# First loads of a windowed-attention and SiLU feed-forward kernel: q/k rows in four loads with a shared leftover tile, v blocks in two, the first w_in chunk in halves

## The chip, the cores and the metric

The kernel runs on one core of a Trainium2 chip. The metric is the device time of one launch in microseconds: 320.09 us, the median of six runs (318.83 to 320.32). The core has the engines PE (TensorE, matmuls and transposes), DVE (VectorE), ACT (ScalarE), POOL (GpSimd) and SP (SyncE). They run side by side, each in the order of its own program, and wait for each other by semaphores. Loads are moved by 16 DMA engines; here nearly all loads are issued by POOL, since they also turn f32 into f16.

## The reference

```python
B, H, S, D = 8, 8, 576, 64
scores = 1/sqrt(D) * q @ k.T
rel = pos[:, None] - pos[None, :]
mask_plain = (rel >= 0) & (rel < 32)                        # heads 0..3
mask_dil = (rel >= 0) & (rel < 128) & (rel % 4 == 0)        # heads 4..7
attn_out = softmax(masked scores) @ v
x = attn_out.transpose(0, 2, 1, 3).reshape(4608, 512)
h = x @ w_in                    # 512 x 2048
g = h * 1/(1 + exp(-h))
out = g @ w_out                 # 2048 x 512, f32
```

q, k and v are f32 of shape (8, 8, 576, 64). A query sees 32 keys: the last 32 tokens in a plain head, and every fourth of the last 128 in a dilated one.

## The kernel before

**Tiling.** Each batch has 576 tokens. Plain heads work on six blocks of 96 queries (`QB`), each with 128 keys (32 older and its own). Dilated heads see the tokens as m x 4 (`M` = 144 values of m, `DIL` = 4 residues), in two halves of 72 queries with 128 keys each. Layer 1 of the feed-forward (`h`, line 877) and layer 2 (`y`, line 910) go over groups of 512 tokens (the first 512 in two groups of 256), in f16 with f32 accumulation.

**First three batches.** q and k come as rows with m on partitions. 144 rows don't fit on 128 partitions, so they come as 96 (`MA`) and 48 (`MR`). PE transposes them (`td` for dilated heads, `ta` for plain ones), ACT or DVE copies the result out of PSUM to `kqD`, `kP` and `qP`, and PE makes the scores. From batch 3 on, q and k take another path (through DRAM and transposing DMAs) that the change doesn't touch.

**First batch.** Its loads are written out apart from the others. For k, rows 0 to 95 go to the tile `nat` "k", for q, rows 48 to 143 go to `nat` "q" and rows 0 to 47 to `q_rest`, a view of the tile `xR` 1 that is not otherwise used so early. Dilated heads are issued first (`issue_first(HN, H)`), then identity and band mask are made on POOL, then the plain heads' rows are issued. The k rows 96 to 143 follow later (`k0`, to `nat` "rest"). The v data come in two forms: `vraw`, rows for the dilated heads, in two loads (the second is `r0`), and `vp`, 24 windows of 128 tokens for the plain heads, in seven loads: one window without its first 32 rows, the three others of block 0, and then one load for each of the blocks 1 to 5 (3 to 5 are `v0`). `trans_d0`, `trans_a0` make the scores' operands of the first rows, `trans_d1`, `trans_a1` those of the leftover k rows. The first batch's mask is added on PE by a matmul with the band (line 611).

**Order.** `ORDER` is the order in which POOL issues everything behind these: w_in in four chunks of 512 columns (w0 to w3), batch 1's rows (d1 dilated, p1 plain), its v (r1, v1), and w_out in four pieces (o0 to o3). `c0` is a copy on POOL of the second half of `vraw`. POOL issues a load only when the load eight places before it has landed. The order of PE, ACT and DVE is written by a planner inside the kernel (`Plan`): it starts each step when its rings (PSUM buffers) and due times are ready by its own estimates. The due times come from `LOAD_US` (us for each load), `AT_W0` (when the loads ahead of w_in's stage are in), and the tables `AT_DIL`, `AT_PLAIN`, `AT_VRAW`, `AT_VP`. On the chip each engine simply waits in that order.

Of the kernel before, what the change touches and what calls it, by code (L numbers as in the profile page):

```python
# [9 lines left out]
F16 = mybir.dt.float16  # L10
# [6 lines left out]
def kernel(  # L17
# [9 lines left out]
    nc = tc.nc  # L27
    B, H, S, D = q.shape
    DM, DFF = moe_w_in.shape
    P = 128  # L30
# [24 lines left out]
    ORDER = "k0 r0 v0 w0 w1 c0 w2 w3 d1 p1 r1 o0 v1 o1 o2 o3".split()  # L55
    LOAD_US = {"w": 2.55, "o": 2.55, "d": 3.7, "p": 3.7, "r": 1.4, "v": 2.6, "k0": 0.9, "r0": 1.2, "v0": 2.0, "c0": 0.0}
    AT_W0 = 14.5
# [48 lines left out]
    def nat_of(b, key):  # L106
        i = ("k", "q", "rest").index(key)
        return nats[b % 2][:MA, i * RW : (i + 1) * RW].rearrange("p (h r d) -> p h r d", h=H, r=DIL)
# [5 lines left out]
    def issue_nat(b, h0, h1):  # L114
# [10 lines left out]
    q_rest = xRs[1][:MA].rearrange("p c t -> p (c t)").rearrange(  # L125
        "p (h r d) -> p h r d", h=H, r=DIL
    )

    def issue_part(src, m0, m1, dst, h0, h1):
        rows = src[0].rearrange("h (m r) d -> m h (r d)", r=DIL)  # L130
        nc.gpsimd.dma_start(  # L131
            out=dst[: m1 - m0, h0:h1].rearrange("p h r d -> p h (r d)"), in_=rows[m0:m1, h0:h1]
        )

    def issue_first(h0, h1):
        issue_part(k, 0, MA, nat_of(0, "k"), h0, h1)
        issue_part(q, MR, M, nat_of(0, "q"), h0, h1)
        issue_part(q, 0, MR, q_rest, h0, h1)
# [32 lines left out]
    def v_win(t0, n, step=S * D):  # L171
        flat = v.rearrange("b h s d -> (b h s) d")
        win = flat[t0 : t0 + P]
        return bass.AP(
            tensor=win.tensor, offset=win.offset, ap=[win.ap[0], [step, n], win.ap[1]]
        )
# [4 lines left out]
    def issue_vp_first(half):  # L181
        flat = v.rearrange("b h s d -> (b h s) d")
        vp = vps[0].rearrange("p (h j) c -> p h j c", j=NB)
        if half == 0:
            nc.gpsimd.dma_start(out=vp[W:, 0, 0, :D], in_=flat[:QB])
            nc.gpsimd.dma_start(out=vp[:, 1:, 0, :D], in_=v_win(S - W, HN - 1))
        for j in (1, 2) if half == 0 else (3, 4, 5):
            nc.gpsimd.dma_start(out=vp[:, :, j, :D], in_=v_win(j * QB - W, HN))  # L188

    nc.vector.memset(xRs[1][:MA], 0.0)  # L190
    nc.vector.memset(vps[0][:W, 0, :], 0.0)
    for t in vraws:
        nc.vector.memset(t, 0.0)
    nc.vector.memset(nat_of(0, "rest"), 0.0)
    issue_first(HN, H)
    make_identity(nc, ident)
# [6 lines left out]
    issue_first(0, HN)  # L203
    issue_vraw(0, (0,))
    issue_vp_first(0)
# [5 lines left out]
    for t in vps:  # L211
        nc.vector.memset(t[:, :, D:], 1.0)
    for t in vds:
        nc.vector.memset(t[:, :, :, :, D:], 1.0)
    for t in kPs:
        nc.vector.memset(t[:, :, :W], 0.0)
    nc.vector.memset(kqDs[0][:, :, :, 1, MA:], 0.0)
# [5 lines left out]
    FC = 512  # L223
    wi = moe_w_in.rearrange("(c p) f -> p c f", p=P)
    wo = moe_w_out.rearrange("(c p) m -> p c m", p=P)
    AT = {}
    at = AT_W0
    for what in ORDER:
        kind, n = what[0], int(what[1:])
        if kind == "w":  # L230
            nc.gpsimd.dma_start(
                out=w_in16[:, :, n * FC : (n + 1) * FC], in_=wi[:, :, n * FC : (n + 1) * FC]
            )
        elif kind == "o":
            nc.gpsimd.dma_start(
                out=w_out16[:, 4 * n : 4 * n + 4], in_=wo[:, 4 * n : 4 * n + 4]
            )
        elif what == "k0":
            issue_part(k, MA, M, nat_of(0, "rest"), 0, H)
        elif what == "r0":  # L240
            issue_vraw(0, (1,))
        elif what == "v0":
            issue_vp_first(1)
        elif what == "c0":
            nc.gpsimd.tensor_copy(vds[0][:, 1, :, :, :D], vraws[0][:, 1])
        elif kind == "d":
            issue_nat(n, HN, H)
        elif kind == "p":
            issue_nat(n, 0, HN)
        elif kind == "r":  # L250
            issue_vraw(n)
        else:
            issue_vp(n)
        at += LOAD_US[what if n == 0 and kind in "krvc" else kind]
        AT[what] = at

# [85 lines left out]
    AT_DIL = {0: 6.7, 1: AT["d1"], 2: t2 + 7.0}  # L342
    AT_PLAIN = {0: 11.3, 1: AT["p1"], 2: t2 + 7.0}
    AT_VRAW = {0: 12.2, 1: AT["r1"], 2: t2 + 8.6}
    AT_VP = {0: 14.5, 1: AT["v1"], 2: t2 + 11.4}
    AT_CAST = t2 + 18.0
    AT_REST = AT["k0"]
    AT_V1 = (max(AT["r0"] + 1.2, 18.0), AT["v0"])
    AT_WIN = [AT[f"w{n}"] for n in range(4)]
# [97 lines left out]
    def attention(b):  # L447
# [34 lines left out]
        def kq_dil(n, i, h, rp, c, w):  # L482
            r = slice(i * D, i * D + D)
            if pe_path:
                return kqD[r, h, rp, n ^ (b == 0), c : c + w]
            return kqT[r, n, rp, h * M + c : h * M + c + w]
# [53 lines left out]
        def trans_d0(ring, h):  # L540
            tps = small(ring, [P, 2, MR + 2 * MA], F16, f"td_{b}_{h}")
            for rp in range(2):
                for c0, src in (
                    (0, q_rest), (MR, nat_of(b, "q")), (MR + MA, nat_of(b, "k"))
                ):
                    nc.tensor.transpose(  # L546
                        tps[:, rp, c0 : c0 + MA], src[:, HN + h, 2 * rp : 2 * rp + 2, :],
                        ident[:MA, :MA],
                    )
            step = best(0.40, 0.52)  # L550
            yield step
            copy_on(
                step[0], kqD[:, h].rearrange("p r k m -> p r (k m)")[:, :, : MR + 2 * MA], tps
            )

        def trans_d1(ring):
            tps = small(ring, [P, 2 * HN * MR + MR], F16, f"td1_{b}")
            for n in range(2 * HN):
                h, rp = divmod(n, 2)
                nc.tensor.transpose(  # L560
                    tps[:, n * MR : n * MR + MA],
                    nat_of(b, "rest")[:, HN + h, 2 * rp : 2 * rp + 2, :], ident[:MA, :MA],
                )
            tps = tps[:, : 2 * HN * MR].rearrange("p (h r m) -> p h r m", r=2, m=MR)
            step = best(0.36, 0.45)
            yield step
            copy_on(step[0], kqD[:, :, :, 1, MA:], tps)

        def trans_a0(ring, hp, nm):
            w = MA if nm == "k" else M  # L570
            tps = small(ring, [P, DIL, w], F16, f"ta_{b}_{hp}_{nm}")
            parts = [(0, nat_of(b, "k"))] if nm == "k" else [(0, q_rest), (MR, nat_of(b, "q"))]
            for r in range(DIL):
                for c0, src in parts:
                    for i in range(2):
                        nc.tensor.transpose(
                            tps[i * D : i * D + D, r, c0 : c0 + MA], src[:, 2 * hp + i, r, :],
                            ident[:MA, :MA],
                        )
            step = best(0.47, 0.42) if nm == "k" else best(0.68, 0.56)  # L580
            yield step
            dst = kP[:, hp, W : W + DIL * MA] if nm == "k" else qP[:, hp]
            copy_on(step[0], dst.rearrange("p (m r) -> p m r", r=DIL), tps.rearrange("p r m -> p m r"))

        def trans_a1(ring, hp):
            tps = small(ring, [P, DIL * MR + MR], F16, f"ta1_{b}_{hp}")
            for r in range(DIL):
                for i in range(2):
                    nc.tensor.transpose(
                        tps[i * D : i * D + D, r * MR : r * MR + MA],  # L590
                        nat_of(b, "rest")[:, 2 * hp + i, r, :], ident[:MA, :MA],
                    )
            tps = tps[:, : DIL * MR].rearrange("p (r m) -> p r m", r=DIL)
            step = best(0.28, 0.34)
            yield step
            dst = kP[:, hp, W + DIL * MA :].rearrange("p (m r) -> p m r", r=DIL)
            copy_on(step[0], dst, tps.rearrange("p r m -> p m r"))
# [172 lines left out]
        for key in order:  # L770
# [9 lines left out]
            elif kind == "TA" and b == 0:  # L780
                st = Step(
                    lambda ring, a=a: trans_a0(ring, *a), 0.75 if a[1] == "k" else 1.3, rings,
                    [AT_PLAIN[0]],
                )
            elif kind == "TD" and b == 0:
                st = Step(lambda ring, a=a: trans_d0(ring, *a), 0.25, rings, [AT_DIL[b]])
            elif kind == "TR":
                st = Step(lambda ring: trans_d1(ring), 0.2, rings, [AT_REST])
            elif kind == "TS":
                st = Step(lambda ring, a=a: trans_a1(ring, *a), 0.2, rings, [AT_REST])  # L790
# [27 lines left out]
            elif kind == "V":  # L818
                st = Step(lambda ring, a=a: vd_of(*a), 0.0, (), [AT_V1[0] if b == 0 and a[0] else at_vraw], ())
            elif kind == "P":  # L820
# [3 lines left out]
                    [AT_V1[1] if b == 0 and a[0] > 2 else at_vp] + [steps["S", u] for u in us], ("DVE",),  # L824
# [43 lines left out]
    def layer1(g, deps):  # L868
        w = GROUPS[g][1]

        def l1(ring, f):
# [4 lines left out]
            for c in range(HP):  # L876
# [18 lines left out]
                list(deps) + [AT_WIN[f // 4]], ("ACT", "DVE"),  # L895
# [123 lines left out]
```

The softmax here doesn't subtract the row's maximum and nothing guards it: scores larger than these inputs give would overflow.

## Time and profile before

| what | value |
|---|---|
| median of six runs | 320.09 us (318.83 to 320.32) |
| the profiled execution's own time, its span | 320.19 us, 318.5 us |
| granted TensorE clock, mean | 0.989 |
| busy: PE, DVE, ACT, POOL | 301.5, 196.1, 164.0, 57.9 us |
| first transpose, first matmul of layer 1 | 6.86, 20.93 us |
| wait before the first matmul of layer 1 | 2.18 us, for w_in |
| first matmul of layer 2 | 41.41 us, after 0.96 us of waiting for w_out |
| batch 2's first transposes | 57.74 us; 0.33 us of waiting at 58.28 |
| stretch at half clock | 21.6 to 28.5 us |

The profile is of one execution. The span goes from the first to the last instruction; the run's time is 1.7 us longer. All starts are in us from the beginning of the span. "Busy" of PE is modelled for overlapping matmuls, so it may be above the real load. An idle time is put down to what ended last before it. The granted clock is the share of PE's clock that the chip let through.

### The profile page before, as it was taken

How to read it: one execution, taken by the hardware profiler on the slowest of the kernel's cores; microseconds unless marked ns; L12 is line 12 of the kernel's file. 1: busy time of each engine (PE TensorE's matmuls, PEld its weight loads, DVE VectorE, ACT ScalarE, POOL GpSimd, SP SyncE). 2: the span in 40 equal slices, each digit the busy share in tenths (PEclk: the TensorE clock that was granted, in tenths of full speed). 3: DMA queues.
4: the chain of work that ended last, by engine and by line, in shares of the span. 5: the costliest groups of instructions: out<-in, count | busy, mean ns of one | idle time of the engine just before them, and what ended most of it. 6: DMA issues, size and time to landing. Idle time of an engine off the chain costs nothing.

```text
span 318.5 us, 6150 instructions
## 1 busy us (share of the span) xinstructions
PE 301.5 (95%) x2402; PEld 154.6 (49%) x2402; DVE 196.1 (62%) x493; ACT 164.0 (51%) x300; POOL 57.9 (18%) x92
## 2 busy tenths in 40 slices
PE   1978979999999999999999999999999999999994
PEld 1647856555545444544444454444444444444441
DVE  6437989698879768843895787548841552355000
ACT  6755766477765355443653564546452453355111
POOL 8972924000900041005000500000000000000000
PEclk9987999999999999999999999999999999999999
DMA  7999999999999959998999898952181000100221
GB/s 90 153 190 198 159 196 192 212 185 177 112 205 225 201 106 196 179 227 153 195 244 195 134 204 179 191 114 71 54 183 38 31 33 33 66 35 0 84 82 66
DMA packets 106693, 44.51 MB, mean 140 GB/s; under 512 B 73384, under 2 KB 102056, under 8 KB 106664
## 3 DMA queue, kind: packets, MB, share of 16 engines
q0 software_dynamic: 48528, 19.92, 51.8%
q1 hardware_dynamic: 52952, 14.75, 24.6%
q10 hardware_dynamic: 5184, 9.44, 8.8%
q8 instruction: 19, 0.31, 0.4%
q14 instruction: 10, 0.08, 0.1%
HBM read 39.84 MB, written 18.28 MB: 182 GB/s over the span
## 4 chain that ended last, share of the span: by engine, by line
PE 82%; DMA 10%; POOL 4%; issue 1%; DVE 1%; ACT 1%; POOLq 0%
PE y L910 37%; PE h L877 36%; DMA nat<-in_q_dram 5%; PE s L623 3%; DMA w_out<-in_moe_w_out_dram 3%; PE av_d L672 2%; DMA w_in<-in_moe_w_in_dram 2%; PE av_p L672 2%; POOL vp L188 1%; POOL nat L131 1%; POOL vraw L166 1%; DVE oD L676 0%; PE td L529 0%; POOL xR L131 0%; ACT th L886 0%
## 5 line engine op out<-in xcount | busy, mean ns | idle before, releaser
L910 PE MATMUL y<-w_out,gT 128*128 128x512 f16 x576 | 138.5, 379 | 1.3 <-DMA w_out<-in_moe_w_out_dram 1.3
L888 DVE SCALAR_TENSOR_TENSOR gT<-th,h 128x512 f16<-128x512 f32 (+1 forms) x160 | 98.3, 628 | 63.0 <-ACT th L886 62.9
L886 ACT ACTIVATE th<-h 128x512 f32<-128x512 f32 (+1 forms) x160 | 88.5, 555 | 85.9 <-PE h L877 81.1
L877 PEld LDWEIGHTS <-w_in 128*128 128x128 f16 x640 | 59.1, 98 | 55.8 <-DMA w_in<-in_moe_w_in_dram 2.3
L910 PEld LDWEIGHTS <-gT 128*128 128x128 f16 x576 | 53.7, 98 | 60.7 <-issue 1.5
L877 PE MATMUL h<-xR,w_in 128*128 128x512 f16 x320 | 77.9, 379 | 0.1
L877 PE MATMUL h<-xA,w_in 128*128 128x512 f16 (+1 forms) x320 | 66.2, 343 | 2.6 <-DMA w_in<-in_moe_w_in_dram 2.2
L921 ACT ACTIVATE ob<-y 128x512 f32<-128x512 f32 x36 | 21.5, 597 | 42.5 <-PE y L910 42.4
L632 ACT ACTIVATE probs<-s 128x768 f16<-128x768 f32 (+2 forms) x47 | 36.2, 771 | 12.6 <-PE s L623 10.0
L676 DVE TENSOR_TENSOR oD<-av_d,rcps 72x256 f16<-72x256 f32 x64 | 26.9, 421 | 2.2
L672 PEld LDWEIGHTS <-probs 128*128 128x128 f16 x448 | 21.9, 99 | 12.7 <-ACT probs L636 0.7
L676 DVE TENSOR_TENSOR oP<-av_p,rcps 96x256 f16<-96x256 f32 x48 | 20.2, 421 | 1.6
L408 POOL COPY fence<-kqT 128x1 f16<-128x1 f16 x10 | 2.4, 250 | 93.5 <-DMA kqT<-kq_s 93.5
L672 PE MATMUL av_d<-vd,probs 128*128 128x65 f16 x256 | 14.9, 196 | 1.5 <-DVE rcps L675 0.6
L675 DVE RECIPROCAL rcps<-av_p 96x4 f32<-96x4 f32 x48 | 8.3, 174 | 11.7 <-PE av_p L672 11.6
L675 DVE RECIPROCAL rcps<-av_d 72x4 f32<-72x4 f32 x64 | 11.0, 172 | 5.6 <-PE av_d L672 5.6
L641 DVE TENSOR_TENSOR probs<-probs,mask_p 128x768 f16<-128x768 f16 x21 | 11.6, 552 | 4.0 <-ACT probs L632 3.8
L672 PE MATMUL av_p<-vp,probs 128*128 128x65 f16 x192 | 13.0, 197 | 0.0
L641 DVE TENSOR_TENSOR probs<-probs,mask_d 128x576 f16<-128x576 f16 (+1 forms) x23 | 11.8, 513 | 1.0 <-ACT probs L632 0.8
L166 POOL DMA_DIRECT2D vraw<-in_v_dram x16 | 10.8, 678 | 5.6 <-DVE oD L676 2.1
L179 POOL DMA_DIRECT2D vp<-in_v_dram x7 | 10.3, 1474 | 1.9 <-PE h L877 1.8
L546 PE MATMUL td<-ident,xR 96*128 96x96 f16 x8 | 1.9, 276 | 6.9 <-DMA xR<-in_q_dram 6.9
(94 smaller groups left out, 155.0 us busy)
## 6 DMA issues: line engine op xcount, KB each, us to landing
out_dram<-ob ACTq DMA_DIRECT2D x36, 256.0 KB, 3.0
kq_s<-in_k_dram POOLq DMA_DIRECT2D x5, 576.0 KB, 10.4
kq_s<-in_q_dram POOLq DMA_DIRECT2D x5, 576.0 KB, 13.1
vp<-in_v_dram POOLq DMA_DIRECT2D x7, 384.0 KB, 7.8
w_in<-in_moe_w_in_dram POOLq DMA_DIRECT2D x4, 512.0 KB, 9.5
w_out<-in_moe_w_out_dram POOLq DMA_DIRECT2D x4, 512.0 KB, 12.5
vraw<-in_v_dram POOLq DMA_DIRECT2D x8, 224.0 KB, 5.2
x_s<-oP SPq DMA_DIRECT2D x10, 144.0 KB, 3.4
```

Source lines behind the costliest of these rows:

```text
L166: nc.gpsimd.dma_start(out=vraw[p0 : p0 + m1 - m0, ab].rearrange("p h r d -> p h (r d)"), in_=src[m0:m1],)
L179: nc.gpsimd.dma_start(out=vps[b % NV][:, :, :D], in_=v_win(b * H * S - W, HN * NB, QB * D))
L632: nc.scalar.activation(p2, both[:, :, :n], AF.Exp, scale=scale)
L641: nc.vector.tensor_tensor(p2, p2, mk, ALU.mult)
L672: nc.tensor.matmul(a[:, i, : D + 1], lhs(i), rhs(i), start=True, stop=True)
L675: nc.vector.reciprocal(rcp[:n], a[:n, :, D : D + 1])
L676: nc.vector.tensor_tensor(o, a[:n, :, :D], rcp[:n, :, None].broadcast_to([n, HN, D]), ALU.mult)
L877: nc.tensor.matmul(h[:, :w], w_in16[:, c, f * P : (f + 1) * P], x_g[:, c], start=(c == 0), stop=(c == HP - 1),)
L886: nc.scalar.activation(th[:, :w], h[:, :w], AF.Tanh, scale=0.5)
L888: nc.vector.scalar_tensor_tensor(gTs[g][:, f, :w], th[:, :w], 1.0, h[:, :w], ALU.add, ALU.mult)
L910: nc.tensor.matmul(y, gTs[g][:, f, tb * P : (tb + 1) * P], w_out16[:, f], start=(f == 0), stop=(f == NFF - 1),)
L921: nc.scalar.activation(ob, y, AF.Copy, scale=0.5)
```

## The change

Rows 0 to 95 of both k and q now go to `nat` "k" and "q", and rows 96 to 143 of both go to `nat` "rest" (k at partitions 0 to 47, q at 48 to 95), in two loads, so `q_rest` is gone. The four row loads are issued one behind the other ahead of identity and band. The dilated and plain transposes of the first rows become fewer, and the leftover transposes carry k and q together, with two copies out instead of one for plain heads. The v blocks come as one load of the first window and one of the 23 others, ahead of everything in `ORDER`. The first w_in chunk is loaded as two halves of 256 columns, with a due time for each, and `c0` stands behind them, ahead of w1. Clearing memsets stand in another order. The planner's estimates are other ones.

```diff
-    ORDER = "k0 r0 v0 w0 w1 c0 w2 w3 d1 p1 r1 o0 v1 o1 o2 o3".split()
-    LOAD_US = {"w": 2.55, "o": 2.55, "d": 3.7, "p": 3.7, "r": 1.4, "v": 2.6, "k0": 0.9, "r0": 1.2, "v0": 2.0, "c0": 0.0}
-    AT_W0 = 14.5
+    ORDER = "k0 r0 w0a w0b c0 w1 w2 w3 d1 p1 r1 o0 v1 o1 o2 o3".split()
+    LOAD_US = {"w": 2.75, "o": 2.6, "d": 3.7, "p": 3.7, "r": 1.4, "v": 2.6, "k0": 2.0, "r0": 1.2, "c0": 0.0, "w0a": 1.4, "w0b": 1.4}
+    AT_W0 = 10.6
...
         issue_part(k, 0, MA, nat_of(0, "k"), h0, h1)
-        issue_part(q, MR, M, nat_of(0, "q"), h0, h1)
-        issue_part(q, 0, MR, q_rest, h0, h1)
+        issue_part(q, 0, MA, nat_of(0, "q"), h0, h1)
...
-    def issue_vp_first(half):
+    def issue_vp_first():
         flat = v.rearrange("b h s d -> (b h s) d")
...
-        for j in (1, 2) if half == 0 else (3, 4, 5):
-            nc.gpsimd.dma_start(out=vp[:, :, j, :D], in_=v_win(j * QB - W, HN))
+        nc.gpsimd.dma_start(out=vps[0][W:, 0, :D], in_=flat[:QB])
+        nc.gpsimd.dma_start(out=vps[0][:, 1:, :D], in_=v_win(QB - W, HN * NB - 1, QB * D))
...
     issue_first(HN, H)
+    issue_first(0, HN)
     make_identity(nc, ident)
...
-    issue_first(0, HN)
     issue_vraw(0, (0,))
-    issue_vp_first(0)
+    issue_vp_first()
...
+            f0, f1 = {"": (0, 4), "a": (0, 2), "b": (2, 4)}[what[2:]]
+            cols = slice((4 * n + f0) * P, (4 * n + f1) * P)
+            nc.gpsimd.dma_start(out=w_in16[:, :, cols], in_=wi[:, :, cols])
...
             issue_part(k, MA, M, nat_of(0, "rest"), 0, H)
+            issue_part(q, MA, M, nat_of(0, "rest")[MR:], 0, H)
...
-    AT_DIL = {0: 6.7, 1: AT["d1"], 2: t2 + 7.0}
-    AT_PLAIN = {0: 11.3, 1: AT["p1"], 2: t2 + 7.0}
-    AT_VRAW = {0: 12.2, 1: AT["r1"], 2: t2 + 8.6}
-    AT_VP = {0: 14.5, 1: AT["v1"], 2: t2 + 11.4}
+    AT_DIL = {0: 5.4, 1: AT["d1"], 2: t2 + 7.0}
+    AT_PLAIN = {0: 7.5, 1: AT["p1"], 2: t2 + 7.0}
+    AT_VRAW = {0: 8.6, 1: AT["r1"], 2: t2 + 8.6}
+    AT_VP = {0: 10.6, 1: AT["v1"], 2: t2 + 11.4}
...
-            tps = small(ring, [P, 2, MR + 2 * MA], F16, f"td_{b}_{h}")
+            tps = small(ring, [P, 4, MA], F16, f"td_{b}_{h}")
...
+            for n, dst in enumerate((kP[:, hp, W:], qP[:, hp])):
+                step = best(0.27, 0.22)
+                yield step
+                copy_on(
+                    step[0], dst[:, DIL * MA :].rearrange("p (m r) -> p m r", r=DIL),
+                    tps[:, :, n * MR : n * MR + MR].rearrange("p r m -> p m r"),
+                )
```

## The prediction

> **What bounds the kernel now.** I read the page's busy rows first, then PE's waits up to 58.3 us, the chain, the Pool timeline of the loads, and last a table of stretches.
>
> The page: TensorE (PE) is busy 95% of the span; the granted clock has one dent, in slices 3 and 4.
>
> ```profile
> PE 301.5 (95%) x2402; PEld 154.6 (49%) x2402; DVE 196.1 (62%) x493; ACT 164.0 (51%) x300; POOL 57.9 (18%) x92
> PE   1978979999999999999999999999999999999994
> PEclk9987999999999999999999999999999999999999
> ```
>
> PE's waits before 58.3 us. After that PE never waits for a load, so the end moves by as much as PE's work at 58 us is earlier.
>
> ```profile
> PE td L546 <- DMA xR<-in_q_dram: 6.9, 1, 6.9
> PE h L877 <- DMA w_in<-in_moe_w_in_dram: 2.2, 1, 2.2
> PE y L910 <- DMA w_out<-in_moe_w_out_dram: 1.3, 2, 1.0
> PE td L529 <- DMA nat<-in_q_dram: 0.3, 1, 0.3
> ```
>
> The chain of waits (start, length, what): from Pool's v loads at 12.3 to PE at 58.3 three loads carry most of it. One queue of transfers sets the start.
>
> ```profile
> 12.32 1.47 POOL vp L188 x2
> 13.79 7.10 DMA w_in<-in_moe_w_in_dram
> 32.59 8.78 DMA w_out<-in_moe_w_out_dram
> 41.65 16.50 DMA nat<-in_q_dram
> ```
>
> Pool's timeline (start, length): a load of 3 or 4 v windows costs Pool 0.77 us like a load of eight times the bytes.
>
> ```profile
> 4.80 0.69 POOL L131 DMA_DIRECT2D nat<-in_k_dram  x1
> 7.88 0.77 POOL L186 DMA_DIRECT2D vp<-in_v_dram  x1
> 8.64 1.53 POOL L188 DMA_DIRECT2D vp<-in_v_dram  x2
> 33.33 1.44 POOL L179 DMA_DIRECT2D vp<-in_v_dram  x1
> ```
>
> Stretches (bounds; length and busy us of PE, PEld, DVE, ACT, POOL; clock; DMA share; GB/s). The queue moves 191 GB/s when full, 94 after Pool's stop at 3.4 to 4.8, 97 and 123 where small v loads ran it dry. The clock halves for 6.8 us after the stretch with the 2.2 us wait (PE busy 1.23 of 3.41).
>
> ```profile
> 3.75:6.00 2.25, 0.00 (x0) 0.00 (x0) 2.06 (x6) 1.77 (x5) 2.11 (x6) 1.00 1.43 191
> 6.00:7.00 1.00, 0.14 (x3) 0.18 (x4) 0.91 (x9) 1.00 (x4) 1.00 (x3) 1.00 0.91 94
> 7.00:10.00 3.00, 3.00 (x36) 2.26 (x34) 0.56 (x2) 2.40 (x6) 3.00 (x5) 1.00 1.32 162
> 10.00:12.00 2.00, 2.00 (x58) 1.61 (x56) 0.00 (x0) 1.71 (x5) 2.00 (x4) 1.00 1.80 136
> 12.00:12.75 0.75, 0.26 (x13) 0.15 (x8) 0.47 (x1) 0.75 (x3) 0.71 (x2) 1.00 1.09 97
> 14.75:15.75 1.00, 1.00 (x30) 0.90 (x24) 0.93 (x5) 0.67 (x2) 0.54 (x1) 1.00 2.23 167
> 16.00:17.00 1.00, 1.00 (x21) 0.59 (x20) 0.86 (x3) 1.00 (x4) 1.00 (x2) 1.00 1.25 123
> 18.21:21.62 3.41, 1.23 (x18) 0.69 (x14) 0.52 (x3) 1.01 (x3) 3.02 (x6) 1.00 1.24 203
> 21.62:25.03 3.41, 2.81 (x33) 1.99 (x32) 1.58 (x6) 1.82 (x5) 0.80 (x2) 0.50 1.25 210
> 38.69:42.10 3.41, 2.44 (x32) 1.65 (x31) 3.40 (x11) 2.70 (x6) 1.10 (x2) 1.00 2.09 173
> ```
>
> **The change part by part.** Bytes are those written to SBUF (f16), as the page counts KB.
>
> *Issue on Pool.* The seven v block loads took 0.53 + 0.77 + 5 x 0.76 = 5.1 us; the two new ones take 0.53 and 23/24 of the 1.44 of a 24-window load, 1.9 us. Two xR loads (0.57 each) go and one leftover q load (0.65) comes. So 3.7 us of issue leave ahead of w_in, and one 0.76 comes (w_in in halves). The four row loads now stand together ahead of identity and band (1.45 us of Pool): the stop falls while 0.98 us each of loads 2 to 4 is still queued. Identity is ready at 1.38 + 0.79 + 3 x 0.68 + 0.6 = 4.8, before its data; the masks end about 0.5 later than now (6.6), and their first reader stood at 8.73: hidden.
>
> *The queue.* The first load lands at 1.38 + 3.8 = 5.2 as before. Behind it up to the end of the first w_in chunk come 983 KB of q/k rows, 393 KB of dilated v, 389 KB of v blocks and 524 KB of w_in, 2289 KB, the same bytes in both kernels. Before they took 15.7 us (chunk landed at 13.79 + 7.1 = 20.9), 146 GB/s. With the queue never dry: rows and dilated v 1376 / 191 = 7.2 us; w_in halves, which now also have 512-byte pieces, 524 / 191 = 2.7; the v blocks at the 136 GB/s of 10 to 12 us, where small pieces prevail, 2.9. Sum 12.8, landing at 18.0: 2.9 us sooner. The 23-window load is not in the trace of before; bounds: all 2289 KB at 136 GB/s, 16.8 us, landing 1.1 later than now; and everything as above with the v blocks at 167 GB/s (14.75 to 15.75), 3.4 sooner. I take 2.9, because the three stretches that made the mean low each have a cause that the change removes; at 162 GB/s for the rows (7 to 10 us, whose cause I don't know) it would be 1.6.
>
> *The copy of the second dilated v half* (c0, 1.04 us on Pool) now stands between the w_in halves and chunk 1 and holds the four remaining w_in and batch-1 loads behind it. Its data land at 18.0 - 2.7 = 15.3, it ends at 16.3, and first bytes follow an issue by some 1.5 us (1.38 to 2.8): 17.8, with the queue occupied until 18.0. Cost nothing, by 0.2 us of cover; if those v rows land later, the halves behind them do too.
>
> *PE before w_in.* It starts when q lands (about 6.2), not xR (6.7). Eight transposes fewer for the dilated heads (24 took 2.07 us, so 0.7), sixteen fewer for plain q (32 took 0.7, so 0.35). The split leftovers add two copies of 192 columns (0.35 each) on ACT or DVE. New waits, in PE's order: the first plain AV needs the whole v block load, 5.2 + (590 + 164) / 191 + 2.9 = 12.0, with PE there at about 13.5 (behind DVE's four reciprocal and multiply pairs, 0.54 each); the leftover transposes need both leftover loads, 12.0 + 393 / 191 = 14.1, with PE there at about 14; everything behind them waits too. From there to the last masked scores took 15.03 to 18.75, so 17.8, and 3.0 us more (four h groups of 0.43, scores, AV) bring PE to the fifth h group at 20.8; chunk 1 lands at 18.0 + 2.6 = 20.6. So the gains in PE's own work are worth nothing: chunks 1 to 3 pace it, and up to a microsecond of PE lateness is hidden too.
>
> *After w_in.* The order and bytes of the loads are unchanged, and the lag of eight loads that Pool observes (its waits at 21.2, 23.7, 27.1, 30.1) moves along. So batch 1's dilated rows land at 32.4 - 2.9 = 29.5, the first w_out piece at 41.4 - 2.9 = 38.5, batch 2's rows at 58.1 - 2.9 = 55.2. PE: 5.5 us of work lie between the fifth h group at 20.8 and batch 1's transposes, so it idles some 3 us in the waits for chunks 2, 3 and those rows (before, the half clock filled that time). From the transposes to the first w_out matmuls 7.5 us passed; 37.0, so it waits for w_out with 1.5 to spare. From about the fifth group of tokens on the built programs have the same order on PE, and no work is added anywhere behind.
>
> *Sum.* 2.9 us off the profiled execution's 320.19 (span 318.5): 317.3. That execution stands 0.1 above the median, which I leave.
>
> **A rule against the trace, twice.** The Trainium skill, "DMA: Bandwidth & Descriptors", section "Anatomy of one DMA", gives each load a fixed 2.0 us besides its bytes; by that the halved w_in chunk would pay one more, 319.3. In this trace chunk 1 landed 2.5 us after chunk 0, its bytes alone, so with loads queued the fixed part overlaps.
> The page "TensorE: Matmul & The Clock Gate", section "Why this matters for your kernels", asks only that PE have no idle gap over about 3 us; by that none of the new waits drops the clock, 317.3. The row 18.21 speaks against it: one 2.2 us wait in a thinly used stretch was enough.
>
> **The rivals.**
> *The clock drops later.* For: the three waits (up to 1.5 us before batch 1's rows) may leave a stretch of 3.41 us with PE under half busy, and 1.23 dropped it. Against: 2.44 busy (38.69) did not; the bound lies between. Then 6.8 us at half clock from about 29 lose 3.4 us of work; 1.5 are spare, PE reaches w_out at 40.4, 1.0 sooner than before, and the two later waits of 0.33 give up to 0.7 back: 318.5 to 319.2. An earlier drop is covered by w_in.
> *The queue stays slow (the slower side).* One mechanism: the 2,944-piece v load, ahead of all of w_in, holds the queue at the rate of small pieces. At 136 GB/s throughout, w_in lands 1.1 later and the same shift goes through: 321.3. It decides at 146 GB/s; under 139 it is slower by over 0.3%. For: 162 GB/s even in row loads. Against: 191 to 205 whenever loads were queued.
> *Hidden anyway.* The w_out pieces keep their time, because Pool's waits hold them: then only w_in's wait shortens, and PE waits at 41.4 instead: 320.2. For: Pool waits four times there. Against: each wait is on a load that comes earlier itself.
>
> **How the numbers follow.** The forecast 0.55; clock 0.20; slow queue 0.13; hidden 0.12. One measurement tells about 0.3%, 0.96 us, from no change: under 319.1 is faster, over 321.0 slower. Forecast and most of the clock case are faster, with a fifth of the hidden case: 0.75. Same: half the slow queue, most of the hidden case, 0.14. Slower: 0.11, the rest of those and a clock that stays down longer than 8 us. The forecast's own range is 316.7 (v blocks at 167) to 318.6 (1.6 sooner); 316.0 to 320.2 holds eight in ten, with a little below 316.7 for loads denser than any row.
>
> **What would show it.** Right: the first w_in half lands near 16.6 and the second near 18; no PE wait over 1 us before the first h; short waits for chunks and batch 1's rows; w_out's wait ends near 38.5, batch 2's rows' near 55. The clock case: 0.50 in a stretch after 28. Slow queue: GB/s near 140 from 8 to 16 us. Wrong altogether: a PE wait over 2 us at the v blocks or the leftovers, or a load wait after 56.

## The result and the profile after

| | median | range, runs |
|---|---|---|
| before | 319.78 us | 318.47 to 323.63, 65 |
| after | 320.57 us | 319.66 to 323.57, 28 |

The ratio of after to before is 1.0029, 95% interval 1.0015 to 1.0043: about 0.9 us slower, where 2.8 us faster was forecast. (The ratios leave out disturbed executions, the medians do not, so the two can differ a little.) The profiled execution of the changed kernel took 320.72 us, its span is 319.0; that of before took 320.19. Between these two executions the difference is 0.5 us.

The page of the changed kernel, answering to the first lines shown of before: PE's busy time fell from 301.5 to 300.4 us, and the clock has no dent.

```profile
PE 300.4 (94%) x2378; PEld 153.0 (48%) x2378; DVE 196.2 (62%) x493; ACT 163.8 (51%) x300; POOL 54.7 (17%) x87
...
PE   2887799999999999999999999999999999999994
...
PEclk9999999999999999999999999999999999999999
```

PE's waits in the changed kernel up to 60 us (total, times, longest). The 2.2 us wait for w_in is now three shorter ones, as forecast, but there is a wait of 1.6 us for batch 1's rows and one of 1.2 us for DVE.

```profile
PE td L532 <- DMA nat<-in_k_dram: 5.1, 1, 5.1
PE h L861 <- DMA w_in<-in_moe_w_in_dram: 2.2, 3, 1.0
PE td L518 <- DMA nat<-in_q_dram: 1.6, 1, 1.6
PE ta_k L558 <- DMA nat<-in_k_dram: 1.2, 1, 1.2
PE h L861 <- DVE gT L872: 1.2, 1, 1.2
```

The chain of waits of the changed kernel (start, length, what). Where before it ran through the v block loads and the first w_in chunk, it now runs through the second half of the dilated v, then through Pool itself, then through batch 1's rows.

```profile
6.73 1.50 POOL vp L179
9.46 7.79 DMA vraw<-in_v_dram
18.34 2.18 POOL w_in L221 x3
20.52 1.86 POOL nat L120 x3
22.39 10.43 DMA nat<-in_q_dram
```

Pool's timeline in the changed kernel (start, length). Everything up to the w_in halves is issued by 11.7, 3.6 us earlier than the first two chunks before. Then Pool stands idle for 5.61 us in front of the copy c0 (L232), and chunk 1 is issued behind it at 18.29 only. Before, chunk 1 was issued by 15.29.

```profile
6.72 1.50 POOL L179 DMA_DIRECT2D vp<-in_v_dram  x1
...
9.46 0.74 POOL L161 DMA_DIRECT2D vraw<-in_v_dram  x1
10.16 1.53 POOL L221 DMA_DIRECT2D w_in<-in_moe_w_in_dram  x2
17.30 1.04 POOL L232 COPY vd<-vraw 128x1024 f16<-128x1024 f16 x1 [5.61 <-DMA vraw<-in_v_dram]
18.29 2.23 POOL L221 DMA_DIRECT2D w_in<-in_moe_w_in_dram  x3
```

Stretches of the changed kernel (columns as in the prediction; the last is GB/s). The v blocks' stretch is faster than before (165), w_in's halves run at 198, and then, from 17.5 to 20.5, the DMA engines move 59 GB/s: nothing is queued but the rest of the second half, until chunk 1, issued at 18.29, begins to move.

```profile
8.00:11.00 3.00, 2.26 (x28) 1.20 (x28) 0.40 (x1) 1.41 (x4) 3.00 (x6) 1.00 1.61 134
11.00:14.00 3.00, 3.00 (x44) 1.95 (x42) 1.34 (x6) 1.85 (x5) 0.69 (x1) 1.00 1.74 165
14.00:17.50 3.50, 2.86 (x50) 1.88 (x50) 2.17 (x9) 2.54 (x5) 0.20 (x1) 1.00 1.45 198
17.50:20.50 3.00, 3.00 (x60) 2.21 (x61) 1.46 (x7) 2.78 (x10) 3.00 (x5) 1.00 0.59 59
20.50:23.50 3.00, 2.24 (x30) 1.46 (x28) 2.86 (x11) 2.32 (x7) 3.00 (x6) 1.00 1.18 192
```

The slow stretch in steps of one us:

```profile
18.50:19.50 1.00, 1.00 (x30) 0.68 (x26) 0.32 (x2) 1.00 (x5) 1.00 (x2) 1.00 0.29 39
19.50:20.50 1.00, 1.00 (x24) 0.91 (x17) 0.38 (x2) 1.00 (x5) 1.00 (x3) 1.00 0.62 29
20.50:21.50 1.00, 1.00 (x15) 0.57 (x14) 0.93 (x4) 0.85 (x4) 1.00 (x3) 1.00 1.11 180
```

The kernel before has full speed at 17.5 to 20.5, and its slow stretches earlier:

```profile
11.00:14.00 3.00, 2.51 (x73) 1.94 (x67) 1.41 (x5) 2.52 (x7) 2.96 (x5) 1.00 1.48 137
14.00:17.50 3.50, 3.39 (x69) 2.32 (x67) 2.90 (x12) 2.96 (x7) 2.98 (x4) 1.00 1.62 156
17.50:20.50 3.00, 1.13 (x24) 0.58 (x18) 1.20 (x4) 1.42 (x4) 3.00 (x6) 1.00 1.23 198
```

So the time won at 11 to 17.5 us is given back at 17.5 to 20.5. The landings in one table (us from the span's start; the forecast's by its rates, from its text or worked out as it says; the last column is the first experiment below):

| landing of | before | forecast | after | c0 late |
|---|---|---|---|---|
| plain heads' k rows (the third row load of the changed kernel) | 8.56 | 7.3 | 8.70 | 8.17 |
| last v block | 17.9 | 12.0 | 14.07 | 14.03 |
| second half of dilated v | 15.76 | 15.3 | 17.25 | 16.25 |
| first w_in chunk (second half) | 20.89 | 18.0 | 19.92 | 19.33 |
| chunk 1 | 23.43 | 20.6 | 23.66 | 21.87 |
| batch 1's dilated rows, last | 32.43 | 29.5 | 32.81 | 30.90 |
| first w_out piece | 41.36 | 38.5 | 40.43 | 38.93 |
| batch 2's rows | 58.14 | 55.2 | 57.57 | 55.70 |

At chunk 1 the changed kernel is 0.2 us behind the kernel before, and at batch 1's rows 0.4. PE's timelines meet there: at 32.95 us it starts on these rows, in the changed kernel after a wait, in the kernel before without one (the half clock had kept it busy). First the changed kernel, then the kernel before:

```profile
32.95 0.63 PE L518 MATMUL td<-ident,nat 96*128 96x96 f16 x11 [1.63 <-DMA nat<-in_q_dram]
```

```profile
32.95 0.68 PE L529 MATMUL td<-ident,nat 96*128 96x96 f16 x12
```

From there on the two stay close: the copy out of the first output tile starts 0.2 us later in the changed kernel (52.89 against 52.73), those from 139 to 245 us 0.3 later, and those from 255 us on 0.55 (from 69 to 131 us the two orders have their output tiles at other places). Batch 2's rows land 0.57 us earlier than before, but the changed kernel does not wait for them; PE starts on them at 57.92. Behind 58 us it waits for other engines instead, where the kernel before had only its 0.3 us for these rows:

```profile
PE y L894 <- ACT ob L905: 0.6, 1, 0.6
PE h L861 <- DVE gT L872: 0.2, 1, 0.2
```

### The profile page after: what moved, and what is told of

Same layout as the page of the kernel before. It is cut to its first block, busy times and chain, and to the rows that moved or that the text cites. A ratio compares the mean times of both kernels' runs of the same rounds, so it can differ in the third digit from the quotient of the medians.

```text
span 319.0 us, 6092 instructions
## 1 busy us (share of the span) xinstructions
PE 300.4 (94%) x2378; PEld 153.0 (48%) x2378; DVE 196.2 (62%) x493; ACT 163.8 (51%) x300; POOL 54.7 (17%) x87
## 3 DMA queue, kind: packets, MB, share of 16 engines
q0 software_dynamic: 48960, 19.92, 51.5%
## 4 chain that ended last, share of the span: by engine, by line
PE 83%; DMA 6%; POOL 4%; DVE 3%; ACT 1%; issue 1%; ACTq 0%; DVEq 0%; POOLq 0%
PE y L894 38%; PE h L861 36%; PE s L607 3%; DMA nat<-in_q_dram 3%; DMA vraw<-in_v_dram 2%; PE av_p L656 2%; PE av_d L656 2%; POOL nat L127 1%; DVE gT L872 1%; ACT ob L905 1%; POOL w_in L221 1%; POOL nat L120 1%; DVE kqD L481 0%; DVE kP L481 0%; POOL vp L179 0%
## 5 line engine op out<-in xcount | busy, mean ns | idle before, releaser
L861 PEld LDWEIGHTS <-w_in 128*128 128x128 f16 x640 | 58.1, 97 | 57.5 <-issue 3.3
L861 PE MATMUL h<-xA,w_in 128*128 128x512 f16 (+1 forms) x320 | 65.4, 337 | 3.5 <-DMA w_in<-in_moe_w_in_dram 2.2
L616 ACT ACTIVATE probs<-s 128x768 f16<-128x768 f32 (+2 forms) x47 | 36.5, 776 | 19.5 <-PE s L607 16.9
L656 PEld LDWEIGHTS <-probs 128*128 128x128 f16 x448 | 22.2, 99 | 11.7 <-issue 0.3
L656 PE MATMUL av_d<-vd,probs 128*128 128x65 f16 x256 | 14.2, 196 | 0.2 <-ACT qP L479 0.2
L481 DVE COPY vd<-vraw 128x1024 f16<-128x1024 f16 x14 | 7.1, 509 | 3.7 <-DMA vraw<-in_v_dram 3.7
```

What stands on the lines that cost most here:

```text
L616: nc.scalar.activation(p2, both[:, :, :n], AF.Exp, scale=scale)
L656: nc.tensor.matmul(a[:, i, : D + 1], lhs(i), rhs(i), start=True, stop=True)
L861: nc.tensor.matmul(h[:, :w], w_in16[:, c, f * P : (f + 1) * P], x_g[:, c], start=(c == 0), stop=(c == HP - 1),)
```

## The experiments

**The copy c0 behind all of w_in.** PE's order is that of the changed kernel.

```diff
-    ORDER = "k0 r0 w0a w0b c0 w1 w2 w3 d1 p1 r1 o0 v1 o1 o2 o3".split()
+    ORDER = "k0 r0 w0a w0b w1 w2 w3 c0 d1 p1 r1 o0 v1 o1 o2 o3".split()
```

> The changed kernel with the copy c0 moved on Pool from behind the w_in halves to behind chunk 3; every other engine's order is the same. Theory (the copy held w_in: Pool stood from 11.7 to 17.25 us until the second dilated v half had landed, and the queue ran dry from 17.9 to 20.5): chunk 1 lands 3.75 us after the second half now, 2.6 after it here, so near 22.5; batch 1's rows and w_out's first piece come about 1.2 sooner (39.2), PE follows, and the time falls by 0.8 to 1.3 us against the changed kernel, below before. Rival (the lag of the slowest DMA engine sets it, or PE and DVE do): chunk 1 earlier, but w_out's first matmul stays at 40.5 and the time within 0.3 us of the changed kernel.

Measured: 319.04 us (318.14 to 321.59, 12 runs), ratio to before 0.9977 (0.9953 to 1.0000). Against the changed kernel that is 1.5 us by the medians and 2.1 between the profiled executions. Pool's timeline, and the stretch that was dry:

```profile
10.18 2.99 POOL L221 DMA_DIRECT2D w_in<-in_moe_w_in_dram  x4
14.31 0.74 POOL L221 DMA_DIRECT2D w_in<-in_moe_w_in_dram  x1 [1.14 <-DMA vp<-in_v_dram]
16.30 1.04 POOL L232 COPY vd<-vraw 128x1024 f16<-128x1024 f16 x1 [1.25 <-DMA vraw<-in_v_dram]
```

```profile
17.50:20.50 3.00, 3.00 (x60) 2.24 (x57) 1.46 (x7) 2.76 (x10) 2.93 (x5) 1.00 1.29 206
```

206 GB/s where it was 59, and chunk 1 lands 2.54 us after the first one, not 3.74. PE starts on batch 1's rows at 31.03, 1.92 earlier than in both other kernels, and is 1.8 to 2.1 us ahead of the changed kernel at every output tile from the first on. About 0.6 of that the edit doesn't explain: the second half landed at 19.33 and not at 19.92, with the same loads in front of it. So the place of c0 is shown to cost the changed kernel about 1.5 us, with this order of PE, ACT and DVE.

**The changed kernel with the due times of the kernel before.** The loads are issued as in the changed kernel; the planner writes another order.

```diff
-    LOAD_US = {"w": 2.75, "o": 2.6, ..., "r0": 1.2, "c0": 0.0, "w0a": 1.4, "w0b": 1.4}
-    AT_W0 = 10.6
+    LOAD_US = {"w": 2.55, "o": 2.55, ..., "r0": 2.1, "c0": 0.0, "w0a": 1.3, "w0b": 1.25}
+    AT_W0 = 14.5
...
-    AT_DIL = {0: 5.4, ...}; AT_PLAIN = {0: 7.5, ...}; AT_VRAW = {0: 8.6, ...}; AT_VP = {0: 10.6, ...}
+    AT_DIL = {0: 6.7, ...}; AT_PLAIN = {0: 11.3, ...}; AT_VRAW = {0: 12.2, ...}; AT_VP = {0: 14.5, ...}
```

> The changed kernel with the due times that the planner had before (first w_in chunk at 21.15, rows at 6.7 and 11.3, v at 12.2 and 14.5); loads and their order are the changed ones. Theory (order: the new due times promise data 1 to 3 us before they land and so gave PE and DVE an order with a wait of 0.6 us for an output copy near 118 us and one of 1.2 us for DVE at 39 us): these two waits go, 0.5 to 1.0 us off the changed kernel. Rival (the loads alone set it): within 0.3 us of the changed kernel, w_in chunk landings the same as there in both cases.

Measured: 319.62 us (318.41 to 321.41, 12 runs), ratio 0.9988 (0.9961 to 1.0015): 0.95 under the changed kernel, by intervals that just touch. The loads land as in the changed kernel (second half 20.06, chunk 1 23.93, w_out 40.4), which points to the order. Its profiled execution, 321.25 us, is 1.6 above its median and says nothing of the gain's place.

**Seven v block loads again, in the changed kernel's place for them.**

```diff
-        nc.gpsimd.dma_start(out=vps[0][:, 1:, :D], in_=v_win(QB - W, HN * NB - 1, QB * D))
+        vp = vps[0].rearrange("p (h j) c -> p h j c", j=NB)
+        nc.gpsimd.dma_start(out=vp[:, 1:, 0, :D], in_=v_win(S - W, HN - 1))
+        for j in range(1, NB):
+            nc.gpsimd.dma_start(out=vp[:, :, j, :D], in_=v_win(j * QB - W, HN))
```

> The changed kernel with the v blocks in seven loads again (one window, three, then five of four windows), in the same place. Theory (small v loads cost Pool 3.2 us of issue and run the queue dry): rows behind them land later by up to 1 us, Pool waits for c0's data later, w_in later by about 1, time 0.5 to 1.2 us above the changed kernel. Rival (the queue is held by its slowest engine and by c0, not by issue): second dilated v half at 17.3 as now, time within 0.3 us.

Measured: 322.55 us (321.79 to 322.94, 7 runs), ratio 1.0072 (1.0046 to 1.0099): 2.0 us above the changed kernel, more than the 0.5 to 1.2 that were expected. The v blocks themselves land no later (14.11). What is lost is Pool's time: w_in is issued from 13.18 on instead of 10.16, and behind the v blocks the queue runs dry:

```profile
11.00:14.00 3.00, 3.00 (x52) 2.24 (x51) 1.29 (x6) 1.68 (x5) 3.00 (x6) 1.00 1.30 88
```

88 GB/s where one load gives 165; the second half of w_in lands at 21.80 instead of 19.92. The part of the forecast that spoke of Pool's issue is right. In this kernel's profile the clock was halved from 16.7 to 23.5 us; what that adds to the 2.0 us was not measured apart.

**The kernel before with its v blocks in two loads**, in the place where the first of the seven stood; PE's order is that of before.

```diff
-        vp = vps[0].rearrange("p (h j) c -> p h j c", j=NB)
         if half == 0:
-            nc.gpsimd.dma_start(out=vp[W:, 0, 0, :D], in_=flat[:QB])
-            nc.gpsimd.dma_start(out=vp[:, 1:, 0, :D], in_=v_win(S - W, HN - 1))
-        for j in (1, 2) if half == 0 else (3, 4, 5):
-            nc.gpsimd.dma_start(out=vp[:, :, j, :D], in_=v_win(j * QB - W, HN))
+            nc.gpsimd.dma_start(out=vps[0][W:, 0, :D], in_=flat[:QB])
+            nc.gpsimd.dma_start(out=vps[0][:, 1:, :D], in_=v_win(QB - W, HN * NB - 1, QB * D))
```

> The kernel before with its v blocks in two loads, in the place of the first three blocks; the order on PE, ACT and DVE is the one before. Theory (issue of small loads was what the queue lost before w_in): the stretches at 97 and 123 GB/s go, first w_in chunk near 19.9 instead of 20.9, and since PE's order is kept, 0.3 to 1.0 us off the time. Rival (landing is set by the slowest engine): first chunk stays at 20.9, time within 0.3 us; or the whole v load comes later than its first blocks did, PE waits for it near 15 us, and the time rises by up to 0.5.

Measured: 319.57 us (318.38 to 320.74, 12 runs), ratio 0.9996 (0.9971 to 1.0020). The first chunk lands at 20.35 instead of 20.89, half-way between the two expectations, batch 2's rows at 56.68 instead of 58.14; PE waits 0.6 for the v blocks, which land at 15.56. Alone, this part is worth nothing that the time can tell: the 2.0 us of the third experiment hold in the changed kernel only.

**c0 late, and due times equal to the landings measured with it**; beside the first experiment's `ORDER`:

```diff
-    LOAD_US = {"w": 2.75, "o": 2.6, ..., "k0": 2.0, "r0": 1.2, "c0": 0.0, "w0a": 1.4, "w0b": 1.4}
-    AT_W0 = 10.6
+    LOAD_US = {"w": 2.55, "o": 2.55, "o0": 3.6, ..., "k0": 1.5, "r0": 0.8, "c0": 0.0, "w0a": 2.0, "w0b": 1.05}
+    AT_W0 = 14.0
...
-    AT_DIL = {0: 5.4, ...}; AT_PLAIN = {0: 7.5, ...}; AT_VRAW = {0: 8.6, ...}; AT_VP = {0: 10.6, ...}
+    AT_DIL = {0: 6.3, ...}; AT_PLAIN = {0: 9.1, ...}; AT_VRAW = {0: 10.0, ...}; AT_VP = {0: 14.0, ...}
```

> The changed kernel with c0 behind chunk 3 and with due times set to the landings measured there (rows 6.3 and 9.1, dilated v 10.0, v blocks 14.0, leftovers 15.5, w_in 18.3, 19.35, 21.9, 24.45, 27.0, w_out from 38.9); same loads, another order on PE, ACT and DVE. Theory (the early due times cost about a microsecond in waits for DVE at 39 us and for an output copy near 52 and 118 us): 0.5 to 1.2 us below the c0-late kernel's 319.0. Rival (those waits are an accident of each order, and another order has others): within 0.5 us of it, either side.

Measured: 320.14 us (318.38 to 324.83, 12 runs), ratio 0.9975 (0.9945 to 1.0005), as c0 late alone. Due times equal to the landings brought nothing that the time can tell: the waits for loads became waits for DVE (1.4 us in front of a transpose) and for the leftover rows (1.4). In this profile, too, the clock was halved, from 15.9 to 22.7 us.

**The kernel before with the due times of the changed kernel.**

```diff
-    LOAD_US = {"w": 2.55, "o": 2.55, ..., "k0": 0.9, "r0": 1.2, "v0": 2.0, "c0": 0.0}
-    AT_W0 = 14.5
+    LOAD_US = {"w": 2.75, "o": 2.6, ..., "k0": 2.0, "r0": 1.2, "v0": 0.05, "c0": 0.0}
+    AT_W0 = 10.6
...
-    AT_DIL = {0: 6.7, ...}; AT_PLAIN = {0: 11.3, ...}; AT_VRAW = {0: 12.2, ...}; AT_VP = {0: 14.5, ...}
+    AT_DIL = {0: 5.4, ...}; AT_PLAIN = {0: 7.5, ...}; AT_VRAW = {0: 8.6, ...}; AT_VP = {0: 10.6, ...}
...
-    AT_V1 = (max(AT["r0"] + 1.2, 18.0), AT["v0"])
+    AT_V1 = (AT["r0"] + 1.2, AT["v0"])
```

> The kernel before with the changed kernel's due times; its loads and their order are untouched. Theory (the new due times alone cost about 0.9 us, by the difference of the two kernels with the changed loads): 0.5 to 1.3 us above before, with PE in longer waits for v blocks and leftovers ahead of 20 us or new waits for DVE and ACT later. Rival: within 0.3 us, the cost came only together with the changed loads.

Measured: 323.93 us (321.75 to 326.12, 6 runs), ratio 1.0121 (1.0080 to 1.0162). Of PE's waits with it, the three longest behind the first rows:

```profile
PE td L529 <- DMA nat<-in_q_dram: 3.4, 2, 1.9
PE h L877 <- DVE oP L676: 1.4, 1, 1.4
PE y L910 <- DMA w_out<-in_moe_w_out_dram: 1.3, 1, 1.3
```

An order written for loads several us earlier than they come costs the kernel before 4.1 us, far more than the 0.5 to 1.3 that were expected. So the changed kernel's due times alone can lose more than the whole change was to bring; on its own, earlier loads they lose less (0.95, the second experiment).

**The plain heads' q and k rows read from the dilated heads' addresses** (so the plain heads' attention comes from the wrong heads' q and k): does the third row load lag because of where it reads? One execution.

```diff
+        s0 = HN if (h0, h1) == (0, HN) else h0
-            out=dst[: m1 - m0, h0:h1]..., in_=rows[m0:m1, h0:h1]
+            out=dst[: m1 - m0, h0:h1]..., in_=rows[m0:m1, s0 : s0 + h1 - h0]
```

> The changed kernel with the plain heads' q and k rows read from the dilated heads' addresses again (their attention is computed from the wrong heads' q and k); all sizes, queues and orders are as they were. It asks why the third row load landed at 8.7 us and not at 7.1. Theory (first reads of new memory hold one DMA engine): the third and fourth loads land near 7.1 and 8.1. Rival (the lag comes from the time or the queue, not from the addresses): near 8.5 and 9.5 again.

Measured: 321.2 us; third and fourth row load land at 8.55 and 9.63 (8.70 and 9.72 in the changed kernel). So the addresses don't explain it.

**c0 late, with the first w_in chunk whole.**

```diff
-    ORDER = "k0 r0 w0a w0b w1 w2 w3 c0 d1 p1 r1 o0 v1 o1 o2 o3".split()
+    ORDER = "k0 r0 w0 w1 w2 w3 c0 d1 p1 r1 o0 v1 o1 o2 o3".split()
-    LOAD_US = {..., "c0": 0.0, "w0a": 1.4, "w0b": 1.4}
+    LOAD_US = {..., "c0": 0.0, "w0": 2.8}
```

> The changed kernel with c0 behind chunk 3 and the first w_in chunk as one load; order on PE, ACT and DVE is the same. It prices the halves. Theory (transfers are bound by their bytes, and halves only double the packets at half the size): chunk 0 complete at 19.2 instead of 19.35, time within 0.3 us of the c0-late kernel's 319.0. Rival (the earlier first half feeds PE): PE waits 0.8 us or so before the first layer-1 matmul, time up to 0.5 above it.

Measured: 319.03 us (317.84 to 321.52, 12 runs), ratio 0.9982 (0.9955 to 1.0009). The chunk lands at 19.51 (its second half at 19.33 before), PE waits 0.4 in front of the first h group. Halving the chunk is worth nothing and costs nothing that the time can tell.

**Both repairs: c0 late and the due times of the kernel before** (those of the second experiment).

```diff
-    ORDER = "k0 r0 w0a w0b c0 w1 w2 w3 d1 p1 r1 o0 v1 o1 o2 o3".split()
+    ORDER = "k0 r0 w0a w0b w1 w2 w3 c0 d1 p1 r1 o0 v1 o1 o2 o3".split()
...
-    AT_W0 = 10.6
+    AT_W0 = 14.5
...
```

> The changed kernel with both repairs: the copy c0 behind the fourth w_in chunk, and the due times of the kernel before (loads of 2.55 us, AT_W0 14.5, AT_DIL 6.7, AT_PLAIN 11.3, AT_VRAW 12.2, AT_VP 14.5), so that the planner writes another order for PE. Each repair alone brought about 319.0 to 319.6 us. If the two losses are separate (1.5 us for Pool's stop before chunk 1, 0.95 us for the order), the sum gives 320.6 - 2.4 = 318.2 us, ratio to the kernel before 0.995. If the order only matters where loads are late (the rival, for which the fifth run speaks, where measured due times added nothing), the time is that of c0 late alone, 319.0 us, ratio 0.998. Both expect chunk 1 to land at about 22 us and chunk 3 at about 27.5.

Measured: 320.32 us (318.68 to 321.67, 12 runs), ratio 0.9998 (0.9968 to 1.0029). The two repairs do not add up: the sum's 0.995 lies outside the interval, the rival's 0.998 in it. By the medians the old due times are 1.3 us worse than the new ones with c0 late (the intervals overlap) and 0.95 better with c0 early. The landings are as expected (chunk 1 at 21.85, w_out at 37.80, earlier than in any other kernel), which points to PE's order again: it waits 1.7 us for DVE's output tiles and 1.1 for `gT`. PE, ACT and DVE have the same order here as in the second experiment, so the two differ by the place of c0 alone: chunk 1 lands 2.1 us sooner, and no gain in time shows (320.32 against 319.62). What c0's place costs depends on the order.

**The changed kernel with its row loads apart again.**

```diff
     issue_first(HN, H)
-    issue_first(0, HN)
     make_identity(nc, ident)
...
+    issue_first(0, HN)
     issue_vraw(0, (0,))
```

> The changed kernel with the plain heads' two row loads issued behind identity and band again, as before; every other instruction is the same. If grouping the four row loads bought what the prediction gave it (the queue no longer dry at 6 to 7 us, the rows at 191 GB/s), undoing it makes the third row load land about 1 us later than its 8.7 us and the second w_in half later than its 19.9, and the time stays or rises by up to 1 us. If grouping bought nothing, because the slowest DMA engine sets the landing of the third load in either place, the third load lands between 8.2 and 9.2 us, w_in's second half within 0.5 us of 19.9, and the time is within 0.3% of the changed kernel's 320.6 us.

Measured: 321.33 us (319.81 to 323.2, 10 runs), ratio 1.0027 (0.9999 to 1.0055), that of the changed kernel. Its third row load is issued 1.43 us later and lands at 8.53, not later. From issue to landing (the last number), in the changed kernel, here, and in the kernel before:

```profile
nat<-in_k_dram POOLq DMA_DIRECT2D x1, 192.0 KB, 5.9
```

```profile
nat<-in_k_dram POOLq DMA_DIRECT2D x1, 192.0 KB, 4.3
```

```profile
nat<-in_k_dram POOLq DMA_DIRECT2D x1, 192.0 KB, 3.8
```

The third load is as the rival had it. The second w_in half lands at 20.72, 0.8 later than in the changed kernel, as the theory had it and outside the rival's 0.5; but the same loads landed 0.6 apart in the first experiment and the changed kernel. By the time, grouping the rows bought nothing that the runs can tell.

**The kernel before with c0 ahead of chunk 1.** Does a copy ahead of a chunk cost its length wherever it stands?

```diff
-    ORDER = "k0 r0 v0 w0 w1 c0 w2 w3 d1 p1 r1 o0 v1 o1 o2 o3".split()
+    ORDER = "k0 r0 v0 w0 c0 w1 w2 w3 d1 p1 r1 o0 v1 o1 o2 o3".split()
```

> The kernel before with the copy c0 ahead of the w_in chunk 1 instead of behind it; all else is the same. In the kernel before, the copy's data land at about 15.8 us, the first chunk only at 20.9. If a copy on Pool between the loads costs time only as far as its data land near the end of what is queued (the theory: in the changed kernel 17.25 us against 17.6, the start of the chunk's last second half), here Pool issues chunk 1 by about 18.5 us, chunk 1 lands at about 23.4 us, at most 0.5 us later than before, and the time is within 0.3% of 319.8 us. If a copy ahead of a chunk costs its 1.04 us wherever it stands (the rival), chunk 1 lands at about 24.5 us and the time is 1 us or more above.

Measured: 320.53 us (317.99 to 322.6, 10 runs), ratio 1.0013 (0.9979 to 1.0047). Pool issues chunk 1 at 17.40, its first chunk lands at 21.28, and chunk 1 at 23.86, 2.58 later. By these landings the copy costs nothing but the bytes. The queue did feel it:

```profile
18.50:19.50 1.00, 0.74 (x16) 0.37 (x14) 0.60 (x2) 0.54 (x2) 1.00 (x2) 1.00 1.02 128
19.50:20.50 1.00, 0.00 (x0) 0.00 (x0) 0.00 (x0) 0.43 (x1) 1.00 (x3) 1.00 0.97 130
```

The kernel before moves 200 and 206 GB/s there. The first DMA engine was done with the first chunk at 18.96, 1.56 us after chunk 1 was issued, and the last, at 21.28, hides the gap. Chunk 1 lands 0.43 us later than before, chunk 2 no later (26.37 against 26.85). So where a whole chunk is still queued in front, the copy costs less than its 1.04 us, but not nothing; the time agrees, though its interval is wider than the 0.3% that was asked.

## Why the prediction was wrong

The end was forecast through batch 1's dilated rows, w_out and batch 2's rows. The first of these landed at 32.81, 3.3 us after the forecast's 29.5, and with that all of the 2.9 was gone. The 3.3 split as follows.

1. **The step "Cost nothing, by 0.2 us of cover" failed, and it turned the sign.** It is 1.1 of the 3.3 us, and with c0 moved the kernel is no longer slower than before. c0's data landed at 17.25, not 15.3; the step had even said that the halves behind them would then be late too, and by its own sum the copy was still covered: it ended at 18.34, 1.5 us to first bytes makes 19.84, and the second half landed at 19.92. The 1.5 us were right, too: chunk 1's first packets came at 19.7, 1.4 us after its issue. What is wrong is the cover itself, at both ends. By the sixteen DMA engines' semaphore increments the first had finished that half at 17.92, nine by 18.29, the last at 19.92, and a load has landed only with the last; from 18.5 to 19.5 the rate is 39 GB/s. Most engines stood empty for up to two us while the load "occupied" the queue. And first bytes are not full rate: from 19.5 to 20.5 it is 29 GB/s, then 180. Chunk 1 came 3.74 us after the half, not 2.6: 1.1 us. Moving the copy gives 1.5 us of time back.
2. **The queue term, 2.9 us, was mis-sized by 1.9, the larger part of the 3.3.** "With the queue never dry: rows and dilated v 1376 / 191" gave 1.4 too little by the third row load, which lands at 8.0 to 8.95 in all kernels, issued anywhere from 2.8 to 4.8. The 162 GB/s of 7 to 10 us, "whose cause I don't know", fits this lag; the 1.6 us worked out from it would have been nearer (1.0 was measured). The v blocks took 3.5 us and not 2.9, 0.6 more. The halves took 2.67, as forecast.
3. **The rest, 0.25 us,** lies between chunk 1 and batch 1's rows (9.15 against 8.9).
4. **"No work is added anywhere behind"**, and with it "the end moves by as much as PE's work at 58 us is earlier", missed that PE, once the loads come early, waits for other engines. Even in the changed kernel batch 2's rows came 0.57 us earlier than before, and the end 0.5 later. With c0 late, batch 2's rows land at 55.70, nearly the forecast's 55.2, and still the time is only 0.7 us under before by the medians (1.6 between profiled executions). PE starts on these rows at 57.43 only, 1.7 us after they landed; it has waited 1.2 us for DVE's `gT` at 36 to 37 us and waits 1.1 in all for ACT's copies into `ob`. The due times are part of this (second, sixth and ninth experiment), but no single rule of them was found: which order fits which loads stays open.

Right were: the 3.7 us of issue that leave ahead of w_in (3.6 measured), of which the v blocks' 3.0 are worth 2.0 us of time in the changed kernel, by the third experiment; the short waits for the chunks and for batch 1's rows; and that the v blocks and leftovers bring no long wait. That PE's own gains before w_in are worth nothing was not tried alone; PE still waits 2.2 us for w_in behind them. Of the rivals, the slow queue was the nearest by its sign, but not by its place: the 23-window load took 0.6 us more than forecast and made PE wait nowhere, the queue was slow in front of it and empty behind w_in.

**The two rules.** Halving a queued chunk cost nothing: its second half landed at 19.33 in the first experiment, the whole chunk at 19.51 in the eighth, with 319.04 and 319.03 us. The Trainium skill, "DMA: Bandwidth & Descriptors", section "Anatomy of one DMA", gives each load a fixed 2.0 us. So it isn't added where loads are queued. Where the queue was dry a fixed part shows: chunk 1 of the changed kernel took 5.4 us from issue to landing, 2.8 more than the 2.54 between queued chunks.

In the changed kernel's profile, with gaps of at most 1.63 us behind the first rows, and with c0 late, with one of 2.02, the clock was full in every slice of the page; the forecast's rival of a dropped clock did not come. The Trainium skill, "TensorE: Matmul & The Clock Gate", section "Why this matters for your kernels", warns of idle gaps over about 3 us. These two kernels agree with it, but others don't: the clock was halved in the kernel before with no gap over 2.18 us behind the first rows, and in the third experiment's kernel with none over 0.81 between 9 us and the drop at 16.7. So the length of one gap does not order these runs.

## What to carry to other kernels

A compute instruction on the engine that issues the loads is a gate for everything behind it: ask when its data land, and put it behind the loads that have to follow closely. Measure its cover against the moment when the first DMA engine runs empty, not against the landing of the last queued load, and count from issue to full rate (over two us here), not to the first bytes (1.4). Time won early on a queue is kept only if the next load is already issued, so follow the issue of each load that paces the end, not just its bytes. And earlier loads are worth only as much as the other engines' order lets through: with c0 late, batch 2's rows came 2.4 us sooner than before and the end 0.7 by the medians.

## What was not expected of the hardware

- One load's DMA engines can finish two to three us apart (6.91 to 8.70 for the third row load, 17.92 to 19.92 for the w_in half, 26.63 to 29.84 for chunk 3 of the kernel before), and loads queued behind keep a spread of this size; behind the dry stretch it is 0.4 us (chunk 1, 23.26 to 23.66). What makes the third load lag is open. Its addresses don't explain it (seventh experiment), and its place in Pool's program isn't shown to: the spread is 1.26 us in the tenth experiment and 1.1 to 2.1 in the kernels with the four row loads together.
- A dry queue takes over two us from issue to full rate: chunk 1 was issued at 18.29, the rate was 29 GB/s from 19.5 to 20.5, 180 in the next us and 206 after that. At the start of the kernel before it was the same: the first load was issued at 1.38, and the row below is followed by the prediction's row of 191 GB/s.

```profile
2.75:3.75 1.00, 0.00 (x0) 0.00 (x0) 0.84 (x2) 0.00 (x0) 0.93 (x4) 1.00 0.68 42
```

- The 6.8 us at half clock cost the kernel before little. In its profile the rows of batch 1 landed at 32.43, so PE, which took them at 32.95, lost 0.5 us at most by then. Of the 81 executions of the kernel before that were run beside the experiments, the 37 with a mean granted clock under 0.993 have a median of 320.45 us, the other 44 one of 319.73.
- The half clock came in eight of the thirteen profiles, for 3.4 or 6.8 us at a time: besides the kernel before in those of the second (17.7 to 24.6), third, fifth, sixth, seventh, ninth and eleventh experiment. The seventh has the changed kernel's order on PE, ACT and DVE and was halved from 17.0 to 20.4 us, the changed kernel itself was not. What triggers it here was not settled.
